# Block attention before two MLP stages: in each pair of heads the second half-tile takes the heads in the other order

## The chip, the cores and the metric

The kernel runs on one core of a Trainium2 chip. TensorE (PE) multiplies matrices, VectorE (DVE) and ScalarE (ACT) work elementwise and empty PSUM, GpSimd (POOL) does the remaining subtractions and the indirect DMAs, SyncE (SP) issues most of the DMAs. The metric is the device time of one launch in microseconds. Three runs of the kernel before took 1456.92, 1457.62 and 1458.24 us; their median is 1457.62 us.

## What is computed

Attention inside chunks of 64 positions, for 8 batches, 8 heads, 576 positions and a head size of 64; then a dense layer pair, then a layer pair of eight experts with one expert per token. Only the first part is touched:

```python
q_c, k_c, v_c = (a.reshape(B, H, nc, chunk, D) for a in (q, k, v))     # chunk = 64
scores = scale * np.matmul(q_c, k_c.transpose(0, 1, 2, 4, 3))
scores = scores - np.max(scores, axis=-1, keepdims=True)
attn = np.exp(scores)
attn = attn / (np.sum(attn, axis=-1, keepdims=True) + 1e-09)
out = np.matmul(attn, v_c)
x = out.transpose(0, 2, 1, 3).reshape(B * S, H * D)
...
h = x @ w_in;  g = s * relu(h) ** 2 + b;  y = g @ w_out
...
# expert of each token by argmax, then relu(y @ w1[e]) @ w2[e], scaled by the gate
```

## The kernel before

**Tiles and blocks.** The 4608 tokens are 36 tiles of 128 rows (two chunks of 64 each); two tiles make a block of 256 tokens, and there are 18 blocks. The 8 heads of a tile are four pairs `hp` (KC = 4). Attention of a tile has these steps: `a_transpose` (queries and keys are turned, so that the head size lies on the partitions: head 0 of a pair on partitions 0 to 63, head 1 on 64 to 127), `a_scores`, `a_soft` and `a_norm` (softmax, on DVE and ACT), `a_pt` (the probabilities are turned), `a_pv` (probabilities times values). `a_pv` leaves the result in `x0` and `x1` (a rounded high part and the rest), the moving operand of the first dense layer `l1_mm`.

**The small products.** A score or value product is 64x64x64. It occupies one quarter of the array: the row half is given by the partitions that its operands lie on, the column half by the partitions that it writes. In `a_scores` each pair makes four products, for head `r` and chunk `c`: row half `r`, column half `c`, so all four quarters come up, and the result of head `r` goes into the PSUM part `sc[r]`. In `a_pv` each pair makes four products too, for chunk `c` and head `r`: `vs` holds the values of head `r` on partition half `r`, the transposed probabilities of head `r` are on half `r` as well, and the result goes to partition half `r`. So the row half always equals the column half, and only two of the four quarters come up. All 16 results of a tile go into one PSUM tile `ps` of 128x512 f32, named `pxt`; heads 0 and 1 of one pair and chunk write the same 64 columns, on the two partition halves. Then one ACT copy (128x512) makes the high part and one DVE subtraction (128x512) the rest. Each product is an f32 matmul and stands in the trace as two matmul instructions, so that each of the two steps has 32 of them per tile.

**PSUM slots.** `pxt`, the transposed probabilities `ppt`, the small rank sums `prk` (`g_rank`), the column sums `pcs` (`c_sums`), the turned rows `pyt` and the narrow forms of the queries and keys and scores all come from one pool, `ps_1`, which has two buffers. They are given out in turn: a new tile takes the buffer of the tile given out two before it, and its first matmul waits until that one has been read.

**Order.** The program's order is written out by hand. Tiles 0 to 3 are done in a start phase in a single chain, together with the first conversions of weights (`c_split`, `c_word`, `c_high`, `c_low` on ACT and DVE, which turn double-precision weights into a high and a low part). Tiles 4 and 5 stand in a loop over `s` that still converts weights and does the dense layers of blocks 0 and 1. Then, for blocks j = 2 to 16, a loop over 16 slices `f` does the dense layers of block j (`m_l1`, `l2_lag`), the routing of block j - 1 (`gates`), the preparation of expert weights (`w_prep`, `w_high`, `w_store`) and the attention of the two tiles of block j + 1: `ATT` gives the slices. `a_pv` of the first tile stands at f = 7 ahead of `a_transpose` of the second, `a_pv` of the second at f = 13; `g_rank` of block j - 1 follows at f = 14. Block 17 and the expert stage have no attention.

Of the kernel before, what the change touches and what calls it, by code (L numbers as in the profile page):

```python
# [8 lines left out]
F32 = mybir.dt.float32  # L9
# [5 lines left out]
AF = mybir.ActivationFunctionType  # L15
ALU = mybir.AluOpType
# [14 lines left out]
def kernel(  # L31
# [16 lines left out]
    nc = tc.nc  # L48
    P = 128
# [3 lines left out]
    E, _, F2 = w1.shape  # L53
    CH = 64
    KC = DM // P
# [19 lines left out]
    def pool(name, bufs=1, side="left", st=None):  # L75
        st = st or ExitStack()
        p = st.enter_context(tc.tile_pool(name=name, bufs=bufs, side=side, reuse_waits="tile"))
        return p, st

    const, _ = pool("const", st=ctx)  # L80
# [3 lines left out]
    ps_1 = ctx.enter_context(tc.tile_pool(name="ps_1", bufs=2, space=PSUM))  # L84
# [19 lines left out]
        out=tri, in_=ones, pattern=[[1, P]], compare_op=ALU.is_gt, fill=0.0,  # L104
# [27 lines left out]
    xt_p, _ = pool("xt", 2, st=ctx)  # L132
    sm, _ = pool("sm", 2, st=ctx)
# [31 lines left out]
    def tt(out, a, b, op):  # L165
        nc.vector.tensor_tensor(out=out, in0=a, in1=b, op=op)  # L166
# [111 lines left out]
    def v_load(i, eng=None):  # L278
        if i >= NTILE:
            return  # L280
        if 0 < i < 3:
            vs = s1.tile([P, 2, KC, HD], F32, name=f"v{i}")
        else:
            vs = (s2 if i in (3, 5) else at).tile([P, 2, KC, HD], F32, tag="v", name="vs")
        for c in range(2):
            b, s = divmod(i * P + c * CH, S)
            for r in range(2):
                (eng or nc.sync).dma_start(
                    out=vs[r * CH:(r + 1) * CH, c],
                    in_=v[b, :, s:s + CH, :].rearrange("(a r) p d -> r p a d", r=2)[r],  # L290
                )
        vt[i] = vs
# [26 lines left out]
    def a_scores(i, narrow=False):  # L319
        qk = qkv[i][0]  # L320
        if narrow:
            sc = [ps_1.tile([P, KC, CH], F32, tag="p1", name="psc1") for _ in range(2)]
            parts = [(slice(r, r + 1), sc[r].unsqueeze(1)) for r in range(2)]
        else:
            ps = ps_2.tile([P, 2, 2, KC, CH], F32, tag="p2", name="psc")
            sc = [ps[:, r, 0] for r in range(2)]
            parts = [(slice(0, 2), ps[:, :, 0])]
        for hp in range(KC):
            for d in range(2):
                for r in range(2):  # L330
                    c = r ^ d
                    r0, c0 = r * CH, c * CH
                    nc.tensor.matmul(
                        sc[r][c0:c0 + CH, hp, :],
                        lhsT=qk[r0:r0 + CH, 0, hp, c0:c0 + CH],
                        rhs=qk[r0:r0 + CH, 1, hp, c0:c0 + CH],
                        start=True, stop=True,
                    )
        qkv[i][0] = parts
# [39 lines left out]
    xt = {}  # L379

    def a_pv(i):
        pt = qkv.pop(i)[1]
        vs = vt.pop(i)
        ps = ps_1.tile([P, KC, P], F32, tag="p1", name="pxt")
        for hp in range(KC):
            for c in range(2):
                for r in range(2):
                    r0, c0 = r * CH, c * CH
                    nc.tensor.matmul(
                        ps[r0:r0 + CH, hp, c0:c0 + CH],  # L390
                        lhsT=vs[r0:r0 + CH, c, hp, :],
                        rhs=pt[r0:r0 + CH, hp, c0:c0 + CH],
                        start=True, stop=True,
                    )
        j, t = divmod(i, NTB)
        if t == 0:
            xt[j] = [xt_p.tile([P, KC, TB], F32R, tag=f"x{a}", name=f"x{a}") for a in range(2)]
        hi, lo = (a[:, :, t * P:(t + 1) * P] for a in xt[j])
        nc.scalar.activation(out=hi, in_=ps, func=AF.Copy)
        tt(lo, ps, hi.bitcast(F32), ALU.subtract)  # L400


    gch = {}
# [619 lines left out]
    def att_pe(j, f, loc):  # L1023
        i = (j + 1) * NTB
        for t, (f0, f1, f2, f3, f4) in enumerate(ATT):
            narrow = i + t == 3 * NTB
            L = LOC[t]
            if f == f0 and L[0] == loc:
                a_transpose(i + t, narrow)
                a_load(i + t + 1)  # L1030
            if f == f1 and L[1] == loc:
                a_scores(i + t, narrow)
                if t:
                    drain(a_soft(i + t))
            if f == f3 and L[2] == loc:
                a_pt(i + t)
            if f == f4 and L[3] == loc:
                a_pv(i + t)
                v_load(i + t + 1)
# [57 lines left out]
    with tc.manual_schedule(engines=ENG):  # L1097
# [8 lines left out]
        c_load(0)  # L1106
        a_load(2)
        v_load(0)
        v_load(1)
        a_load(3)  # L1110
        c_load(1)
# [4 lines left out]
        nc.sync.dma_start(out=sb[:, 1:2], in_=b_in.partition_broadcast(P))  # L1116
        a_transpose(0)
        a_scores(0)
        drain(a_soft(0))
        a_transpose(1)  # L1120
        drain(a_norm(0))
        a_scores(1)
        c_split(0)
        a_pt(0)
# [3 lines left out]
        drain(a_norm(1))  # L1128
        c_high(0)
        a_pv(0)  # L1130
        c_low(0)
        v_load(2, nc.scalar)
# [3 lines left out]
        next(soft)  # L1136
        next(soft)
        a_pv(1)
        drain(soft)
        a_transpose(3)  # L1140
# [32 lines left out]
        for s in range(2, NF + LEAD + LAG):  # L1173
# [52 lines left out]
            if s == 6:  # L1226
                s1_st.close()
                wt_p, _ = pool("wt", st=ctx)
# [15 lines left out]
            if s == 17:  # L1244
                drain(c_sums(15, 16))
                su_st.close()
                y_p, _ = pool("yp", st=ctx)
                gb_p, _ = pool("gb", st=ctx)
                wgb = gb_p.tile([P, E * DM], F32, name="wgb")
                nc.sync.dma_start(  # L1250
                    out=wgb, in_=wgt.rearrange("e d -> (e d)").partition_broadcast(P)
# [4 lines left out]
        g_p, _ = pool("g", 3, st=ctx)  # L1256
# [4 lines left out]
    with tc.manual_schedule(engines=ENG):  # L1261
# [38 lines left out]
        j = NB - 1  # L1300
        xgp, _ = pool("xgp", st=ctx)
        for n in range(3):
            xg_t[n] = xgp.tile([P, ROW], F32, name=f"xg{n}")
        a1, _ = pool("a1", st=ctx)
# [3 lines left out]
        for f in range(NF):  # L1308
            if f == NF - 4:
                wi_st.close()  # L1310
                r3, _ = pool("r3", 2, st=ctx)
                r2, _ = pool("r2", st=ctx)
                uo, _ = pool("uo", st=ctx)
# [37 lines left out]
        r5, _ = pool("r5", st=ctx)  # L1351
# [8 lines left out]
        ut, _ = pool("ut", side="right", st=ctx)  # L1360
# [66 lines left out]
        hi = NU - 2  # L1427
# [49 lines left out]
```

## Time and profile before

| | us |
|---|---|
| median of three runs | 1457.62 |
| the profiled execution, its own time | 1454.87 |
| its span, first to last instruction | 1453.2 |
| PE busy, share of the span | 1408.9, 97% |
| DVE busy | 939.1, 65% |
| ACT busy | 701.0, 48% |
| mean granted clock of TensorE, share of full speed | 0.99 |

The profile is one execution on the chip. For each instruction it has the engine, the line of the kernel, the operation, the tiles and the start and end; from the semaphores it infers what ended an engine's idle time. Matmuls are pipelined, and their ends are modelled; so the cost of a row of matmuls is read from its start to the start of what follows on PE, not from its duration. PE works nearly without a gap from about 70 us on, so what shortens its work there shortens the whole, unless another engine becomes late.

### The profile page before, as it was taken

The page shows a single profiled execution, that of the slowest core. Times are in us where ns is not written, and L with a number is a line of the kernel's source. Part 1 is how long each engine was busy: PE and PEld are TensorE (multiplying, and loading weights), DVE is VectorE, ACT ScalarE, POOL GpSimd, SP SyncE. Part 2 cuts the span into 40 slices and gives each one's busy share as a digit, 9 for nine tenths or more (in the row PEclk, how much of TensorE's full clock was granted, in tenths as well). Part 3 has the DMA queues.
Part 4 walks back from the last instruction along what each step waited for, and adds up shares of the span by engine and source line. Part 5 has one row for each costly group of instructions (what it writes and reads, how often), then busy time and mean ns, then how long its engine had stood idle before and what let it go on. Part 6 is the DMA issues. An engine that isn't in the chain of part 4 may idle for free. (4 is left out here: it accounts for less than half of the span.)

```text
span 1453.2 us, 34204 instructions
## 1 busy us (share of the span) xinstructions
PE 1408.9 (97%) x13165; PEld 1184.1 (81%) x13165; DVE 939.1 (65%) x2279; ACT 701.0 (48%) x1622; POOL 448.1 (31%) x515
## 2 busy tenths in 40 slices
PE   5799999999999999999999999999999999999996
PEld 4698888888888888888888888887777777777773
DVE  5889489779778966876876786766343344344331
ACT  3786556565565555555556555543222222222221
POOL 0000232322232333233233333363543443444320
PEclk8899999999999999999999999999999999999998
DMA  7484253554545445344444534453211221535340
GB/s 174 145 200 126 100 146 115 143 151 139 144 141 149 125 120 145 112 113 126 132 124 111 152 97 118 86 176 111 74 46 52 102 100 47 181 131 196 113 149 19
DMA packets 183893, 179.00 MB, mean 123 GB/s; under 512 B 131108, under 2 KB 139556, under 8 KB 179504
## 3 DMA queue, kind: packets, MB, share of 16 engines
q1 hardware_dynamic: 171216, 157.29, 37.3%
q0 software_dynamic: 10336, 18.97, 4.2%
q8 instruction: 105, 1.72, 0.5%
q10 hardware_dynamic: 2176, 0.52, 0.2%
q14 instruction: 60, 0.49, 0.1%
HBM read 263.85 MB, written 54.14 MB: 219 GB/s over the span
## 5 line engine op out<-in xcount | busy, mean ns | idle before, releaser
L424 POOL TENSOR_TENSOR gl<-g,gh 128x256 fp32r<-128x256 f32 x256 | 222.9, 872 | 700.7 <-ACT gh L422 398.5
L409 PE MATMUL ph<-x,wi 128*128 128x256 f32 x2592 | 348.0, 285 | 5.2 <-ACT wi L232 2.7
L409 PEld LDWEIGHTS ph<-x,wi 128*128 128x128 f32 x2592 | 331.0, 191 | 20.1 <-ACT wi L232 3.4
L482 PE MATMUL py<-wo,gh 128*128 128x512 f32 x864 | 270.7, 394 | 0.0
L540 DVE CUSTOM_DVE_ANT_0 dump<-rows,wgb 128x512 bf16<-128x512 f32 x256 | 198.9, 777 | 5.0
L979 DVE CAST hh<-hr 128x512 f16<-128x512 f32 x82 | 37.4, 456 | 253.4 <-ACT hr L975 253.4
L989 PEld LDWEIGHTS <-hh 128*128 128x128 f16 x984 | 94.6, 98 | 106.7
L419 ACT ACTIVATE g<-ph 128x256 f32<-128x256 f32 x256 | 97.2, 380 | 165.1 <-PE ph L409 156.9
L975 ACT ACTIVATE hr<-pu,scu 128x128 f32<-128x128 f32 x328 | 93.5, 367 | 169.9 <-PE pu L967 87.2
L482 PE MATMUL py<-wo,gl 128*128 128x512 f32 x432 | 170.5, 395 | 0.0
L482 PEld LDWEIGHTS py<-wo,gh 128*128 128x128 f32 x864 | 148.1, 188 | 20.9
L967 PEld LDWEIGHTS <-wa 128*128 128x128 f16 x2208 | 127.0, 98 | 5.5 <-issue 0.3
L967 PE MATMUL pu<-xhl,wa 128*128 128x128 f16 x2208 | 130.6, 219 | 0.0
L718 DVE SCALAR_TENSOR_TENSOR hl<-raw,wup,hl 128x512 f16<-128x512 f32 x128 | 106.7, 873 | 30.8 <-ACT hl L711 30.8
L989 PE MATMUL po<-wa,hh 128*128 128x512 f16 x552 | 122.9, 379 | 0.0
L409 PE MATMUL ph<-x,wj 128*128 128x256 f32 x864 | 116.0, 284 | 1.8 <-DVE wj L166 1.8
L711 ACT ACTIVATE hl<-raw,wup 128x512 f16<-128x512 f32 x128 | 85.1, 711 | 62.3 <-DVE wup L163 40.4
L409 PEld LDWEIGHTS ph<-x,wj 128*128 128x128 f32 x864 | 108.1, 189 | 6.3 <-DVE wj L166 2.0
L996 POOL DMA_INDIRECT out_dram<-o,uid x41 | 42.1, 1028 | 225.0 <-ACT o L995 211.6
L420 ACT ACTIVATE g<-g 128x256 f32<-128x256 f32 x256 | 107.0, 418 | 8.1
L422 ACT ACTIVATE gh<-g 128x256 fp32r<-128x256 f32 x256 | 107.0, 418 | 8.1
L995 ACT ACTIVATE o<-po,scu 128x512 f32<-128x512 f32 x41 | 28.2, 687 | 164.4 <-PE po L989 164.4
(210 smaller groups left out, 2031.3 us busy)
## 6 DMA issues: line engine op xcount, KB each, us to landing
wa<-wd SPq DMA_DIRECT2D x64, 1024.0 KB
wb<-wd SPq DMA_DIRECT2D x60, 1024.0 KB
raw<-in_moe_w_dram SPq DMA_DIRECT2D x64, 512.0 KB
wd<-hl SPq DMA_DIRECT2D x128, 256.0 KB
wb<-wd SPq DMA_DIRECT2D x20, 1030.5 KB
wa<-wd SPq DMA_DIRECT2D x20, 1030.5 KB
ys<-rows SPq DMA_DIRECT2D x18, 513.0 KB
vs<-in_v_dram SPq DMA_DIRECT2D x132, 64.0 KB
```

The source lines that it names most:

```text
L409: nc.tensor.matmul(ps, lhsT=wi_f(a, f)[:, kc], rhs=xt[j][b][:, kc, :], start=(n == 0), stop=(n == 3 * KC - 1),)
L419: nc.scalar.activation(out=g, in_=ps, func=AF.Relu)
L420: nc.scalar.activation(out=g, in_=g, func=AF.Square)
L422: nc.scalar.activation(out=hi, in_=g, func=AF.Copy)
L424: nc.gpsimd.tensor_tensor(out=lo, in0=g, in1=hi.bitcast(F32), op=ALU.subtract)
L482: nc.tensor.matmul(yps[j][t], lhsT=g[a][:, t * P:(t + 1) * P], rhs=wo_f(b, f), start=(f == 0 and n == 0), stop=(f == NF - 1 and n == 2),)
L540: nc.vector.tensor_tensor_reduce(out=dump, in0=ysb[j][:, t, :DM], in1=wgb[:, e * DM:(e + 1) * DM], scale=1.0, scalar=0.0, op0=ALU.mult, op ...
L711: nc.scalar.activation(out=hl[:, 0], in_=raw[:, a], func=AF.Copy, scale=sc)
L718: nc.vector.scalar_tensor_tensor(out=hl[:, 1], in0=raw[:, a], scalar=sc, in1=hl[:, 0], op0=ALU.mult, op1=ALU.subtract)
L967: nc.tensor.matmul(ps[:, f, :], lhsT=w[:, kc, a, f * P:(f + 1) * P], rhs=hl[:, b, kc, :], start=(n == 0), stop=(n == 3 * KC - 1),)
L975: nc.scalar.activation(out=r[:, f, :], in_=ps[:, f, :], func=AF.Relu, scale=scu[:, c:c + 1])
L989: nc.tensor.matmul(ps, lhsT=hh[:, a, c, :], rhs=w[:, c % 4, b, :], start=(n == 0), stop=(n == 3 * NC2 - 1),)
```

## The change

The values of the chunk c = 1 are loaded with the two heads of a pair exchanged: head `r` lies on partition half `r ^ c`. To match, the scores go into the part `sc[d]`, with d = r ^ c, in place of `sc[r]`; so in chunk 1 the two heads of a pair change places in the softmax tile, and after the transposition head `r` of chunk `c` lies on half `r ^ c`. In `a_pv` the operands are taken from half `k0` = (r ^ c) * 64, and the result still goes to half `r`. The products of chunk 0 lie in the quarters in which row half and column half are the same, those of chunk 1 in the two others. The results of the two chunks go into two PSUM tiles of 128x256, both of the pool `ps_1`, and each has its own ACT copy and its own DVE subtraction. Nothing is computed in addition.

```diff
@@ v_load
             for r in range(2):
                 (eng or nc.sync).dma_start(
-                    out=vs[r * CH:(r + 1) * CH, c],
+                    out=vs[(r ^ c) * CH:(r ^ c) * CH + CH, c],
                     in_=v[b, :, s:s + CH, :].rearrange("(a r) p d -> r p a d", r=2)[r],
                 )
@@ a_scores
                     c = r ^ d
                     r0, c0 = r * CH, c * CH
                     nc.tensor.matmul(
-                        sc[r][c0:c0 + CH, hp, :],
+                        sc[d][c0:c0 + CH, hp, :],
                         lhsT=qk[r0:r0 + CH, 0, hp, c0:c0 + CH],
                         rhs=qk[r0:r0 + CH, 1, hp, c0:c0 + CH],
@@ a_pv
-        ps = ps_1.tile([P, KC, P], F32, tag="p1", name="pxt")
+        ps = [ps_1.tile([P, KC, CH], F32, tag="p1", name="pxt") for _ in range(2)]
         for hp in range(KC):
             for c in range(2):
                 for r in range(2):
-                    r0, c0 = r * CH, c * CH
+                    r0, c0, k0 = r * CH, c * CH, (r ^ c) * CH
                     nc.tensor.matmul(
-                        ps[r0:r0 + CH, hp, c0:c0 + CH],
-                        lhsT=vs[r0:r0 + CH, c, hp, :],
-                        rhs=pt[r0:r0 + CH, hp, c0:c0 + CH],
+                        ps[c][r0:r0 + CH, hp, :],
+                        lhsT=vs[k0:k0 + CH, c, hp, :],
+                        rhs=pt[k0:k0 + CH, hp, c0:c0 + CH],
                         start=True, stop=True,
                     )
@@
-        hi, lo = (a[:, :, t * P:(t + 1) * P] for a in xt[j])
-        nc.scalar.activation(out=hi, in_=ps, func=AF.Copy)
-        tt(lo, ps, hi.bitcast(F32), ALU.subtract)
+        for c in range(2):
+            c0 = t * P + c * CH
+            hi, lo = (a[:, :, c0:c0 + CH] for a in xt[j])
+            nc.scalar.activation(out=hi, in_=ps[c], func=AF.Copy)
+            tt(lo, ps[c], hi.bitcast(F32), ALU.subtract)
```

No instruction passes another, but since `a_pv` now takes two slots of `ps_1`, some matmuls wait for other readers than before. Two places show it; the words in square brackets are the engines and DMA queues whose semaphores an instruction waits for. The first is PE at the value product of tile 5, in the loop over `s`, before and after:

```order
L243 MATMUL pcs_1707<-wt0_879,one_157 128x512 [waits Activation_49]
L243 MATMUL pcs_1707<-wt1_880,one_157 128x512
L389 MATMUL pxt_1721<-pt_1672,vs_1101 64x64 [waits DVE_49]
L389 MATMUL pxt_1721<-pt_1672,vs_1101 64x64
L389 MATMUL pxt_1721<-pt_1672,vs_1101 64x64 [waits DMAHW1_49]
L389 MATMUL pxt_1721<-pt_1672,vs_1101 64x64 [waits DMAHW2_49]
L389 MATMUL pxt_1721<-pt_1672,vs_1101 64x64 x12
```

```order
L243 MATMUL pcs_1722<-wt0_891,one_157 128x512 [waits Activation_49]
L243 MATMUL pcs_1722<-wt1_892,one_157 128x512
L391 MATMUL pxt_1736<-pt_1687,vs_1113 64x64 [waits DVE_49]
L391 MATMUL pxt_1736<-pt_1687,vs_1113 64x64
L391 MATMUL pxt_1737<-pt_1687,vs_1113 64x64 [waits DMAHW1_49,DVE_49]
L391 MATMUL pxt_1737<-pt_1687,vs_1113 64x64 [waits DMAHW2_49]
L391 MATMUL pxt_1736<-pt_1687,vs_1113 64x64 x2
L391 MATMUL pxt_1737<-pt_1687,vs_1113 64x64 x2
```

The second of the two tiles, `pxt_1737`, takes the buffer that `pcs` has just filled, and its first matmul waits for DVE, which reads `pcs`. The second place is PE at `g_rank` of block 1, at f = 14 of j = 2, after the value product of tile 7:

```order
L631 LDWEIGHTS ones_85
L631 MATMUL prk_2486<-run_1960,ones_85 128x8 [waits PE_49]
L632 LDWEIGHTS tri_87
L632 MATMUL prk_2486<-oh_2392,tri_87 128x8 [waits DVE_49]
L631 LDWEIGHTS ones_85
L631 MATMUL prk_2486<-run_2394,ones_85 128x8 [waits DVE_49]
```

```order
L635 LDWEIGHTS ones_85
L635 MATMUL prk_2510<-run_1978,ones_85 128x8 [waits DVE_49]
L636 LDWEIGHTS tri_87
L636 MATMUL prk_2510<-oh_2413,tri_87 128x8
L635 LDWEIGHTS ones_85
L635 MATMUL prk_2510<-run_2415,ones_85 128x8
```

Before, `prk` took the buffer of `ppt`; now it takes that of the first `pxt` tile, so its first matmul waits for DVE to have subtracted from it. The same stands in every block from j = 2 to 16.

## Rows read from the trace of the kernel before

**Rows 1.** The page, part 1: busy time of each engine over the span.
```profile
PE 1408.9 (97%) x13165; PEld 1184.1 (81%) x13165; DVE 939.1 (65%) x2279; ACT 701.0 (48%) x1622; POOL 448.1 (31%) x515
```
**Rows 2.** Busy time by stretches of the span; the first line names the columns.
```profile
core 0: us, PE busy (x) PEld busy (x) DVE busy (x) ACT busy (x) POOL busy (x), PEclk, DMA share, GB/s
...
20.00:30.00 10.00, 3.52 (x40) 3.41 (x41) 1.58 (x4) 2.10 (x4) 0.00 (x0) 0.51 0.72 232
...
50.00:60.00 10.00, 7.82 (x47) 6.45 (x46) 8.75 (x16) 9.90 (x20) 0.00 (x0) 0.95 0.53 167
...
200.00:400.00 200.00, 199.16 (x1696) 176.71 (x1695) 164.48 (x417) 118.09 (x264) 60.37 (x69) 1.00 0.52 143
...
930.00:1453.20 523.20, 507.38 (x5458) 384.06 (x5456) 219.41 (x522) 149.45 (x435) 208.84 (x235) 0.99 0.33 106
```
**Rows 3.** Timeline, PE, 249 to 267 us: start, duration, line, tiles, count [idle].
```profile
249.98 1.15 PE L389 MATMUL pxt<-pt,vs 64*64 64x64 f32 x32
251.06 1.69 PE L409 MATMUL ph<-x,wj 128*128 128x256 f32 x12
...
265.53 0.69 PE L333 MATMUL psc<-qk 64*64 64x64 f32 x32 [0.46 <-DVE qk L316]
266.16 0.73 PE L482 MATMUL py<-wt,gh 128*128 128x512 f32 x2
```
**Rows 4.** Matmuls started by 250.08 us (L389) and 265.56 us (L333): count, durations, starts.
```profile
L389 PE MATMUL pxt<-pt,vs x2: 267/267/267, 250.0 to 250.0; 64*64 64x64 f32 x2
...
L333 PE MATMUL psc<-qk x4: 267/267/267, 265.5 to 265.6; 64*64 64x64 f32 x4
```
**Rows 5.** Groups by line and shape: count, busy us, mean ns of one, idle before.
```profile
L419 ACT ACTIVATE g<-ph 128x256 f32<-128x256 f32 x256 | 97.2, 380 | 165.1 <-PE ph L409 156.9 <-POOL gl L424 5.9 <-PE prk L634 0.2
...
L166 DVE TENSOR_TENSOR x<-pxt,x 128x512 fp32r<-128x512 f32 x36 | 24.7, 687 | 36.7 <-ACT x L399 36.6
...
L399 ACT ACTIVATE x<-pxt 128x512 fp32r<-128x512 f32 x36 | 21.2, 589 | 17.2 <-PE pxt L389 17.2
...
L166 DVE TENSOR_TENSOR pr<-psc,mx 128x256 f32<-128x256 f32 x6 | 2.2, 412 | 0.0
```
**Rows 6.** Timeline, 251 to 256 us: DVE's subtraction, and PE's next use of the pool.
```profile
251.81 0.69 DVE L166 TENSOR_TENSOR x<-pxt,x 128x512 fp32r<-128x512 f32 x1
...
255.35 0.18 PE L631 MATMUL prk<-run,ones 128*128 128x8 bf16 x1
```
**Rows 7.** Timeline, DVE and PE at the value product of tile 5.
```profile
151.80 0.69 DVE L166 TENSOR_TENSOR cb<-pcs,cb 128x512 f32<-128x512 f32 x1 [2.27 <-PE pcs L243]
...
151.69 1.15 PE L389 MATMUL pxt<-pt,vs 64*64 64x64 f32 x32
152.77 0.73 PE L482 MATMUL py<-wt,gh 128*128 128x512 f32 x2
```
**Rows 8.** Timeline, DVE and PE, tiles 6 and 7 in block j = 2.
```profile
180.37 0.69 DVE L316 COPY qk<-pqk 128x512 f32<-128x512 f32 x1 [0.31 <-ACT qk L312]
...
203.64 0.69 DVE L166 TENSOR_TENSOR x<-pxt,x 128x512 fp32r<-128x512 f32 x1
...
203.20 0.18 PE L631 MATMUL prk<-run,ones 128*128 128x8 bf16 x1
...
203.63 0.71 PE L482 MATMUL py<-wt,gh 128*128 128x512 f32 x2
```
**Rows 9.** Timeline, PE and ACT in the start phase.
```profile
7.34 1.14 PE L333 MATMUL psc<-qk 64*64 64x64 f32 x32 [0.88 <-DVE qk L316]
...
25.83 0.60 ACT L376 ACTIVATE pt<-ppt 128x512 f32<-128x512 f32 x1 [7.74 <-DMA v<-in_v_dram]
26.48 1.97 PE L389 MATMUL pxt<-pt,v 64*64 64x64 f32 x32 [7.78 <-ACT pt L376]
...
40.22 1.09 PE L372 MATMUL ppt<-ident,pr 128*128 128x128 f32 x4 [3.27 <-DVE pr L166]
...
46.31 0.50 PE L409 MATMUL ph<-x,wi 128*128 128x256 f32 x2 [1.22 <-ACT wi L232]
```

## The prediction

> **What bounds the kernel now.** I read the busy times first, then the stretches, then the timeline around the changed steps, then the start phase. PE is busy for 97% of the span [rows 1]. By stretches it is busy for 199.16 of the 200 us from 200 to 400 us, at full granted clock, while DVE has 164 us of work there and ACT 118 us [rows 2]. All but the first six tiles have their attention in this regime, up to 926 us. So a microsecond taken from PE there is a microsecond of the whole, as long as DVE and ACT are still in time where PE waits for them. The expert stage after 930 us is PE's too [rows 2] and is not touched: it only starts earlier. The first 70 us are different. PE is idle for much of them, its clock falls to a mean of 0.51 in one stretch, and from 50 to 60 us ACT is the full engine [rows 2].
>
> **The value product itself.** In the steady part a value product takes from 249.98 to 251.06 us on PE, 1.08 us. A score product, with the same count and shape of matmuls, takes from 265.53 to 266.16 us, 0.63 us [rows 3]. The difference shows at the front of each: within the first 0.1 us two value matmuls have started, but four score matmuls [rows 4]. 32 matmuls two at a time are 16 groups, four at a time 8 groups, so the 0.45 us of difference are 8 groups of 0.056 us each. The scores use four quarters of the array and the values two; after the change the values use four as well, in the order of the scores (two on the diagonal, then two off it). I therefore give the value product the 0.63 us of the scores: **0.45 us less per tile**.
>
> Does the new placing of results stand against that? Now the two diagonal products of a pair write the same columns of one PSUM tile, on the two partition halves, and the two others do so in a second tile; that holds for the scores as well, which before kept each row half to its own part. The nearest row is the old value product: its heads 0 and 1 write the same columns of `pxt` on the two halves, and both start within the first 0.1 us [rows 4], with the next pair right behind, as 1.08 us for 16 groups say. So two row halves do write into one place at the same time. No row shows this with four in flight. Taken as it stands, the price is 0; at the other end it is 0.45 us per tile for the scores, and no gain for the values (the first rival).
>
> [...]
>
> **Emptying PSUM.** One ACT copy of 128x512 (589 ns) becomes two of 128x256, near 380 ns by the nearest row from PSUM; one DVE subtraction (687 ns) becomes two of about 412 ns [rows 5]. That is 0.17 us more on ACT and 0.14 us more on DVE per tile, 6 and 5 us over 36 tiles. In the steady part both hide behind PE: DVE has 35 us to spare in 200 [rows 2]. And the result is not later: DVE begins after the first, short copy, and the last half is ready after 0.38 + 0.41 + 0.41 = 1.20 us in place of 0.59 + 0.69 = 1.28 us. The loads of the values are the same four DMAs with other target partitions, at no cost.
>
> **The slots.** A value product now takes both buffers of the pool. In blocks 3 to 16 the next use after the second tile's product is the rank sum, and it now waits for DVE's first subtraction. That subtraction starts at 251.81 us, and even the whole of it ends at 252.50 us; the rank sum comes at 255.35 us [rows 6]. The 2.85 us of cover shrink by the 0.45 us saved at most, so the cost is nothing. The scores of the next tile already wait 0.46 us for DVE in one such block [rows 3]; the chain that delays them starts behind the value product and moves with it, so I leave that wait as it is. So **28 tiles (8 to 35) give 28 x 0.45 = 12.6 us**.
>
> Three places are worse. *Tile 5*: its second PSUM tile takes the buffer of the column sums. DVE reads these from 151.80 to 152.49 us, and the value product starts at 151.69 us [rows 7]. The third product must wait until about 152.54 us, 0.85 us after the first; nearly the whole product still follows it, so PE goes on after about 0.85 + 0.63 = 1.48 us where it took 1.08 us: **0.4 us lost** instead of 0.45 us gained. *Tiles 6 and 7*: from 180.37 us to past 204 us DVE works almost without a break, and PE's next needs come out of that row of work. It starts at a copy that waited 0.31 us for ACT [rows 8]; an earlier value product of tile 6 can bring it forward by at most these 0.31 us, less 0.14 us of longer subtraction ahead of it; I take 0.2 us. At its end DVE subtracts tile 7 at 203.64 us, then 203.44 us, and the first half is done at 203.85 us. The rank sum, which began at 203.20 us and let PE go on at 203.63 us [rows 8], now starts at 203.9 us and lets PE go on at 203.98 us. Both tiles together: **0.35 us lost** rather than 0.9 us gained. *Tile 4* has no such neighbour: 0.45 us gained.
>
> **The start phase.** Tile 0: nothing, because ACT is held until 25.83 us by the loads of values [rows 9]. Tile 1 runs while the granted clock is near its lower level (0.51 from 20 to 30 us [rows 2]): 1.97 us, against 1.14 us for scores run that slowly [rows 9], so 0.83 us less, and ACT's next work hangs on it; 0.7 us after ACT's longer copies. Tile 2: the probabilities of tile 3 wait 3.27 us for DVE [rows 9], whose chain begins at this value product: 0.5 us. Tile 3: PE waits for converted weights after it [rows 9], so nothing is gained; there ACT is full [rows 2], and the longer copies cost 0.2 us. Sum 1.0 us gained. As idle PE also moves the granted clock here, I bound it by 0.5 us lost and 2.5 us gained.
>
> **The sum.** 12.6 + 0.45 - 0.4 - 0.35 + 1.0 = 13.3 us. The profiled execution took 1454.87 us, of which 1453.2 us are span, and would take 1441.6 us. It lies 2.75 us below the median of the runs; from the median the forecast is 1457.6 - 13.3 = **1444.3 us**.
>
> **The rivals.**
>
> *Slower, through PSUM.* With four quarters in flight, two row halves that write one tile get in each other's way. Then the scores fall from 0.63 to 1.08 us, and the values stay at 1.08 us: 36 x 0.45 = 16 us more, about 1474 us. It decides as soon as the pair on the diagonal and the pair off it cannot be written together; if it only halves the overlap of both, gain and loss cancel near 1457 us. For it: the scores before kept each row half to its own part, and no row has four in flight in the new way. Against it: the pairs of the old value product. Chance 0.07.
>
> *No four in flight.* The third matmul of each value product carries a new wait, and the loads of the values are waited for one by one; if that keeps the pairs apart, the value product stays at 1.08 us. Then only the losses of tiles 5 to 7 and the start phase remain: 1457 to 1459 us. Against it: the waits are for things long done in the steady part, and the old product had the waits for the loads too. Chance 0.05.
>
> *The slots cost more.* DVE's subtraction comes late not in one block only but in many, because DVE is filled with routing ahead of it. Each block in which the rank sum then waits as in block 2 loses what its second tile gains and 0.35 us more, 0.8 us; seven of the 14 blocks would cost 5.6 us, hence 1450 us, all of them 1455 us. Against it: the 2.85 us of cover [rows 6]. Chance 0.08.
>
> **How the numbers follow.** The forecast keeps 0.80. Its own bounds: at the low end all 36 tiles give 0.45 us and the start phase 1.0 us besides, 17.2 us, 1440.4 us; at the high end a start phase 1.5 us worse than taken and a tenth of the steady gain lost to handing over between products, 10.5 us, 1447 us. The range reaches 1 us below, for a run with a higher clock in the start phase, and up to 1450.5 us to take in the nearer half of the third rival: 1439.5 to 1450.5 us. About 0.2% (2.9 us) is what a measurement of this kernel can tell from no change. Faster by more than that: 0.80 + 0.07 of the third rival = 0.87. Within it: 0.05 + 0.01 = 0.06. Slower: 0.07.
>
> **What would show it.** In the profile of the changed kernel, the steady value product should take 0.63 us to the next start, with four matmuls started in the first 0.1 us, and the scores should still take 0.63 us. The copies should be near 0.38 us and the subtractions near 0.41 us. PE should wait about 0.8 us inside the value product of tile 5, and for DVE ahead of the rank sum of block 1 only. The forecast is wrong if the scores get longer, if the rank sums wait in later blocks, or if the first 70 us change by more than 2.5 us.

## The result and the profile after

The changed kernel takes **1443.11 us** (median of four runs, 1441.65 to 1445.47) against 1457.27 us for the kernel before in the same comparison: ratio 0.9904, 95% interval 0.9890 to 0.9917. The forecast was 1444.3 us. The profiled execution took 1441.65 us, 13.2 us less than the one of before.

The timeline of PE around the value product of tile 9 and the score product of tile 10, as in [rows 3] (start, duration, line, tiles, count):

```profile
247.57 0.69 PE L391 MATMUL pxt<-pt,vs 64*64 64x64 f32 x32
248.20 0.97 PE L413 MATMUL ph<-x,wj 128*128 128x256 f32 x6
...
262.23 0.69 PE L335 MATMUL psc<-qk 64*64 64x64 f32 x32
262.86 0.50 PE L486 MATMUL py<-wt,gh 128*128 128x512 f32 x1
```

The value product now takes 0.63 us from its start to the next matmul, where it took 1.08 us; the score product still takes 0.63 us. The matmuls of the same value product that have started within the first 40 ns, as in [rows 4]:

```profile
L391 PE MATMUL pxt<-pt,vs x4: 267/267/267, 247.6 to 247.6; 64*64 64x64 f32 x4
```

Four, where there were two. The groups of the page and by shape that empty PSUM, as in [rows 1, 5]:

```profile
PE 1391.7 (97%) x13165; PEld 1166.9 (81%) x13165; DVE 942.6 (65%) x2315; ACT 703.2 (49%) x1658; POOL 448.4 (31%) x515
```

```profile
L166 DVE TENSOR_TENSOR x<-pxt,x 128x256 fp32r<-128x256 f32 x72 | 27.0, 416 | 19.4 <-ACT x L403 19.4
...
L403 ACT ACTIVATE x<-pxt 128x256 fp32r<-128x256 f32 x72 | 23.2, 373 | 9.9 <-PE pxt L391 9.9
```

The halves take 416 and 373 ns; DVE and ACT have 3.5 and 2.2 us more work in all. And the waits of PE (waiting tile and line, who is waited for, us in total, times, longest):

```profile
PE psc L335 <- DVE qk L316: 1.8, 2, 1.0
...
PE ppt L374 <- DVE x L166: 1.7, 1, 1.7
PE prk L635 <- DVE x L166: 1.2, 1, 1.2
...
PE px L952 <- DMA xg<-ys,uid: 0.9, 1, 0.9
PE psc L335 <- ACT qk L314: 0.8, 1, 0.8
PE pxt L391 <- DVE cb L166: 0.5, 1, 0.5
PE pqk L307 <- DVE rows L495: 0.5, 1, 0.5
```

Five of these are new: `ppt`, `prk` and `pxt` wait for a slot of the pool, each once; `pqk` waits once for DVE's `rows`; and a score product of the start phase waits once for ACT's `qk`.

How far the second profile is ahead of the first, by the starts of value products:

| place | before, us | after, us | ahead by | gained since the row above |
|---|---|---|---|---|
| tile 4 starts | 137.88 | 135.31 | 2.57 | 2.57 (start phase) |
| tile 5 starts | 151.69 | 148.66 | 3.03 | 0.46 (tile 4) |
| tile 6 starts | 177.53 | 174.82 | 2.71 | -0.32 (tile 5) |
| tile 8 starts | 229.73 | 227.78 | 1.95 | -0.76 (tiles 6 and 7) |
| what follows tile 35 starts | 926.50 | 912.01 | 14.49 | 12.54 (tiles 8 to 35) |
| end of the span | 1453.2 | 1439.9 | 13.3 | -1.2 (expert stage) |

### The profile page after: what moved, and what is told of

Same layout as the page of the kernel before. It is cut to its first block, busy times and chain, and to the rows that moved or that the text cites. A ratio compares the mean times of both kernels' runs of the same rounds, so it can differ in the third digit from the quotient of the medians.

```text
span 1439.9 us, 34299 instructions
## 1 busy us (share of the span) xinstructions
PE 1391.7 (97%) x13165; PEld 1166.9 (81%) x13165; DVE 942.6 (65%) x2315; ACT 703.2 (49%) x1658; POOL 448.4 (31%) x515
## 5 line engine op out<-in xcount | busy, mean ns | idle before, releaser
L722 DVE SCALAR_TENSOR_TENSOR hl<-raw,wup,hl 128x512 f16<-128x512 f32 x128 | 111.1, 908 | 30.3 <-ACT hl L715 30.3
```

The costliest lines, as they stand in the source:

```text
L722: nc.vector.scalar_tensor_tensor(out=hl[:, 1], in0=raw[:, a], scalar=sc, in1=hl[:, 0], op0=ALU.mult, op1=ALU.subtract)
```

## Experiments

**The theory**: the matmuls of one quarter start one after the other, 58 ns apart (the distance of neighbouring starts of one quarter within the value product of tile 9, before and after, at a granted clock of 1.00; only the second comes 0.11 us behind the first), and the gain is that four quarters work at once where two did. The trace gives a product the size 64*64 and no place in the array; a quarter here is the pair of operand half and result half. The score products of the kernel before come in four such pairs, and their matmuls start four at a time, within 0.03 us of one another. **Rivals**: the gain comes from emptying PSUM in two halves; or from where operands and results lie; or the start phase makes much of it by chance.

**One part alone: two PSUM tiles, no exchange of heads** (on the kernel before).

```diff
-        ps = ps_1.tile([P, KC, P], F32, tag="p1", name="pxt")
+        ps = [ps_1.tile([P, KC, CH], F32, tag="p1", name="pxt") for _ in range(2)]
...
-                        ps[r0:r0 + CH, hp, c0:c0 + CH],
+                        ps[c][r0:r0 + CH, hp, :],
...
+        for c in range(2):
...
+            nc.scalar.activation(out=hi, in_=ps[c], func=AF.Copy)
+            tt(lo, ps[c], hi.bitcast(F32), ALU.subtract)
```

> One part alone: two PSUM tiles per value product, with their own copies and subtractions, but the heads stay where they were before, so that only two quarters of the array come up. Theory of the quarters: the value product stays at 1.08 us to the next start in the steady part, two matmuls started in the first 0.1 us; the slots cost what they cost in the changed kernel or a little more (a wait inside the value product of tile 5, one ahead of the rank sum of block 1, together about 1.3 us); time 1457 to 1460 us, ratio 1.000 to 1.002 to the kernel before. Rival (the gain comes from emptying PSUM in two shorter halves): the time falls as in the changed kernel, to about 1443 us, ratio 0.990.

Measured: 1456.32 us against 1455.57 us, ratio 1.0005 (0.9995 to 1.0014). The timeline of PE at the value product of tile 9, and the matmuls started within its first 60 ns:

```profile
252.34 1.15 PE L389 MATMUL pxt<-pt,vs 64*64 64x64 f32 x32
253.42 0.39 PE L411 MATMUL ph<-x,wj 128*128 128x256 f32 x1
```

```profile
L389 PE MATMUL pxt<-pt,vs x2: 267/267/267, 252.3 to 252.3; 64*64 64x64 f32 x2
```

1.08 us and two at a time. Two tiles and shorter copies alone give nothing that these runs can tell; the ratio lies where it was expected, and the time 0.7 us under the expected range (in this comparison the kernel before takes less, too). The extra waits for slots (0.5 us at `pxt`, 0.7 us at `prk` in this profile) are no larger than the interval of the runs. No run has the other part alone, heads exchanged and one PSUM tile; so whether four quarters would work at once into one tile, and the split is needed, stays open.

**The same products in another order** (on the changed kernel): first all of chunk 0, whose quarters are the two on the diagonal, then all of chunk 1.

```diff
-        for hp in range(KC):
-            for c in range(2):
+        for c in range(2):
+            for hp in range(KC):
                 for r in range(2):
```

> The changed kernel with one loop exchanged: in the value product all products of chunk 0 (both on the diagonal) stand ahead of all of chunk 1 (both off it). The same instructions, operands and results, but neighbours share two quarters. Theory of the quarters: 16 groups of two again, the value product takes about 1.08 us, and the steady gain of 0.45 us a tile is lost: 1455 to 1459 us, ratio 0.998 to 1.001. Rival (what counts is where operands and results lie, not which products are neighbours): 0.63 us, about 1443 us, ratio 0.990.

Measured: 1448.66 us, ratio 0.9952 (0.9935 to 0.9969): half of the gain is lost, not all of it. The value product of tile 9 on PE, and the matmuls of it that had started 0.29 us (first line), 0.305 us (second line) and 0.515 us (third line) after its beginning:

```profile
248.26 0.98 PE L391 MATMUL pxt<-pt,vs 64*64 64x64 f32 x32
249.17 0.38 PE L413 MATMUL ph<-x,wj 128*128 128x256 f32 x1
```

```profile
L391 PE MATMUL pxt<-pt,vs x10: 218/218/267, 248.3 to 248.5; 64*64 64x64 f32 x10
...
L391 PE MATMUL pxt<-pt,vs x12: 218/218/267, 248.3 to 248.6; 64*64 64x64 f32 x12
...
L391 PE MATMUL pxt<-pt,vs x22: 218/218/267, 248.3 to 248.7; 64*64 64x64 f32 x22
```

0.91 us, between 0.63 and 1.08 us. Ten have started by 0.29 us, as many as five pairs, and within 15 ns more two others start. The trace has one name for both PSUM tiles, so that these two are of chunk 1 is read from the distance: in one quarter starts lie 58 ns apart. Up to the 22nd both chunks run side by side; the last ten come in pairs again. Each quarter has eight matmuls, so chunk 0 still had six to go when chunk 1 began. The order is what counts, and not the placing alone, since operands and results lie as in the changed kernel; but matmuls of chunk 1 started while six of chunk 0, three in each quarter, had not.

**The same exchange in the scores** (on the changed kernel): all products on the diagonal first.

```diff
-        for hp in range(KC):
-            for d in range(2):
+        for d in range(2):
+            for hp in range(KC):
                 for r in range(2):
```

> The changed kernel with the same exchange in the score product: first all products on the diagonal, then all off it. Theory of the quarters: the score product goes from 0.63 to about 1.08 us in every tile and the value product stays at 0.63 us; 36 x 0.45 = 16 us more than the changed kernel, 1457 to 1461 us. Rival (the pitch of the score product is set by the issue of matmuls or by waiting for its operands): it stays at 0.63 us, about 1443 us.

Measured: 1448.01 us, ratio 0.9948 (0.9932 to 0.9964). The timeline of PE at the score product of tile 10:

```profile
262.09 0.97 PE L333 MATMUL psc<-qk 64*64 64x64 f32 x32 [0.19 <-DVE qk L316]
263.00 0.50 PE L484 MATMUL py<-wt,gh 128*128 128x512 f32 x1
```

0.91 us as well, so the size was missed in the same way and the direction held: what the values gained, the scores lose in part as soon as their neighbours share quarters. The value product stays at 0.63 us in this profile.

**Sorted by quarter** (on the changed kernel), to see how many matmuls of a busy quarter have not started when the next quarter begins:

```diff
-        for hp in range(KC):
-            for c in range(2):
-                for r in range(2):
+        for c in range(2):
+            for r in range(2):
+                for hp in range(KC):
```

> The changed kernel with the products of the value step sorted by quarter: all four of one quarter, then all four of the next. Same instructions and results. From the exchange of loops, where products of a free quarter started while six matmuls of the busy ones were still waiting, I expect a quarter to start when six or fewer are pending ahead of it: 18 groups in place of 8, about 1.2 us for the value product, some 20 us more in all (1460 to 1465 us). Without any overtaking it would be 32 groups, 1.9 us or more, and some 45 us more. Rival (only the placing counts): 0.63 us.

Measured: 1535.1 us, one run, against 1517.14 us for the kernel before on the same chip, hence 30 us more than the changed kernel there (1505.36 us, below). The value product of tile 9 on PE, and the matmuls started 0.283 and 0.288 us after its beginning:

```profile
251.79 1.54 PE L391 MATMUL pxt<-pt,vs 64*64 64x64 f32 x32
253.25 0.38 PE L413 MATMUL ph<-x,wj 128*128 128x256 f32 x1
```

```profile
L391 PE MATMUL pxt<-pt,vs x5: 218/218/267, 251.8 to 252.1; 64*64 64x64 f32 x5
...
L391 PE MATMUL pxt<-pt,vs x6: 218/218/267, 251.8 to 252.1; 64*64 64x64 f32 x6
```

1.46 us, where 1.2 us was expected. Here five have started by 0.283 us and the sixth by 0.288 us; less than 58 ns behind the fifth, it is read as the first of the second quarter, and it starts when the first quarter has three to go, not six. One count fits both orders: three matmuls of each busy quarter had not started when the next quarter began. An estimate from it: if the 32 matmuls in four blocks overlap by three at each of three borders, they make 32 - 9 = 23 groups of 58 ns, 15 more than the 8 of the changed kernel; 15 x 0.058 = 0.87 us, and 0.63 + 0.87 = 1.50 us, near the 1.46 us. By the same count the exchange of loops has 16 - 3 = 13 groups, 5 more than 8, and 0.63 + 5 x 0.058 = 0.92 us, where 0.91 us was measured. The count was made after both runs, to fit them; no run made for it tests it, and what sets it is not shown.

**The changed kernel again, and the kernel before again.** These and the next two runs look at the start phase. The chip on which the kernel before takes 1517 us spends some 60 us more in the expert stage (591 us behind tile 35 in the changed kernel's profile there, 528 us in its first profile), 40 us of it as waits of PE for issue in each profile taken there, so times there are compared with one another alone.

> The kernel before once more, for a second profile of its start phase. If the 2.5 us by which the changed kernel's start phase is shorter belong to the change, the score product of tile 4 starts again near 110.7 us (within 0.5 us) and the granted clock of the first 60 us looks the same; if they are in part the clock's, that start differs by 1 us or more between the two profiles of one kernel.

> The changed kernel once more, beside the next three on one chip, for a second profile and more runs. The steady part should be the same to 0.1 us per block; the score product of tile 4, which started at 108.27 us, may move by about 1 us, as it did between two profiles of the kernel before (110.73 and 109.68 us). Time 1442 to 1445 us.

Measured: the changed kernel 1505.36 us against 1517.14 us, ratio 0.9913 (0.9884 to 0.9943). The score product of tile 4, once per profile, in this order: before, before again, after, after again:

```profile
110.73 0.46 PE L333 MATMUL psc<-qk 64*64 64x64 f32 x16
```

```profile
109.68 0.52 PE L333 MATMUL psc<-qk 64*64 64x64 f32 x20
```

```profile
108.27 0.69 PE L335 MATMUL psc<-qk 64*64 64x64 f32 x32
```

```profile
109.47 0.64 PE L335 MATMUL psc<-qk 64*64 64x64 f32 x28
```

(The counts are those of the part of the product that the asked stretch holds.) Each kernel's start phase moves by more than 1 us from one profile to the next.

**The change from tile 4 on only** (on the changed kernel).

```diff
-                    out=vs[(r ^ c) * CH:(r ^ c) * CH + CH, c],
+                    out=vs[(r ^ (c if i > 3 else 0)) * CH:(r ^ (c if i > 3 else 0)) * CH + CH, c],
...
-                        sc[d][c0:c0 + CH, hp, :],
+                        sc[d if i > 3 else r][c0:c0 + CH, hp, :],
...
+        new = i > 3
...
-                    r0, c0, k0 = r * CH, c * CH, (r ^ c) * CH
+                    r0, c0, k0 = r * CH, c * CH, (r ^ (c if new else 0)) * CH
...
```

> The change from tile 4 on; tiles 0 to 3 as they were before (old placing, one PSUM tile, one copy). If the gain of the start phase belongs to the change, the score product of tile 4 starts near 110.2 us, between the two profiles of the kernel before, and the time is 1.5 to 2.5 us above the changed kernel's; if it was the clock's in the one profile, the start lies anywhere from 108 to 110.7 us and the runs are within 0.5 us of the changed kernel's. The steady part gains 0.45 us a tile either way.

Measured: 1505.06 us, ratio 0.9917 (0.9893 to 0.9941): no difference from the changed kernel that these runs can tell, though with intervals of 0.24% to each side they could not tell the 1.5 to 2.5 us of the one case from the 0.5 us of the other. Its score product of tile 4, in the timeline of PE:

```profile
109.26 0.45 PE L335 MATMUL psc<-qk 64*64 64x64 f32 x15
```

So of the 2.57 us that the first pair of profiles shows for the start phase, most is not shown to be the change's. With the old start phase that start was at 110.73, 109.68, 109.26 and (two tiles only) 110.30 us, with the new placing and order at 108.27, 109.47 and, in the next run, 108.89 us. The means, 110.0 and 108.9 us, are 1.1 us apart, no more than the spread within either, and both chips are mixed in them. The other orders spread wider: 107.16 us with the chunks one after the other, whose value products are slower than the changed kernel's, 107.47 us with the scores exchanged, 110.40 us sorted by quarter.

One part of the start phase is steady, the value product of tile 1 ([rows 9] has it before). The timeline of PE, first in the changed kernel, then in this one:

```profile
26.47 1.23 PE L391 MATMUL pxt<-pt,v 64*64 64x64 f32 x32 [7.40 <-ACT pt L378]
27.64 1.11 PE L307 MATMUL pqk<-ident,q 128*128 128x128 f32 x4
```

```profile
25.29 1.97 PE L396 MATMUL pxt<-pt,v 64*64 64x64 f32 x32 [6.64 <-ACT pt L378]
27.19 1.12 PE L307 MATMUL pqk<-ident,q 128*128 128x128 f32 x4
```

From its start to the next matmul it takes 1.90 us in all four profiles in which tile 1 has the old quarters (the kernel before twice, two tiles only, and this one) and 1.16 us in all four with the new placing and order of the values. These 0.74 us are the change's; how much of them reaches tile 4 is not shown.

**The rank sum of block 1 one slice later** (on the changed kernel), so that DVE is ahead of it.

```diff
-                if f == RANK:
+                if f == (15 if j == 2 else RANK):
                     g_rank(j - 1)
...
-        if f == DEST:
+        if f == (15 if j == 1 else DEST):
             r.append(g_dest(j))
```

> The changed kernel with the rank sum of block 1 (and what DVE makes of it) one slice later, behind the next 2.8 us of matmuls, so that DVE has subtracted from the PSUM tile before PE comes to it. If the 1.2 us wait ahead of that rank sum is a net loss, it is gone (below 0.1 us) and everything behind it starts 1.0 to 1.2 us earlier relative to the value product of tile 7 (29.6 to 29.8 us from there to the rank-sum-free value product of tile 8's block, 32.58 us to tile 8's own before); the runs can hardly tell 0.08%. Rival: the wait moves to the next thing that DVE owes PE, and nothing is gained.

Measured: 1503.26 us, ratio 0.9902 (0.9878 to 0.9925). The timeline of PE at the rank sum, first in the changed kernel's second profile, then in this kernel:

```profile
202.26 0.17 PE L635 MATMUL prk<-run,ones 128*128 128x8 bf16 x1 [1.15 <-DVE x L166]
```

```profile
202.99 0.18 PE L635 MATMUL prk<-run,ones 128*128 128x8 bf16 x1
```

The wait is gone, and none has taken its place: from the value product of tile 7 to that of tile 8 it is 31.19 us (195.25 to 226.44 us), against 32.51 us (195.99 to 228.50 us). That is 1.3 us less than in the changed kernel, a little more than expected, and the lead is still 1.3 us behind tile 35. The runs, with intervals of 0.2 to 0.3% to each side, do not tell the two apart.

## Why the prediction was right, point by point

**The value product.** Forecast 0.45 us less per tile, measured 0.45 us (1.08 to 0.63 us). The reason given was the number of quarters in flight, and the runs bear it out from both sides: the split alone leaves two at a time and gains nothing, and bad neighbours take a part of the gain away while all placing stays. That two row halves write the same columns of one tile, on different partition halves, costs nothing with four in flight either: the score product stays at 0.63 us with its parts exchanged. So the first rival is out. That two row halves write the same partitions of one PSUM part was not tried.

**28 tiles, 12.6 us.** Measured 12.54 us in the first pair of profiles, but that close a hit is luck. The products alone give 28 x 0.454 = 12.7 us. From block 7 to block 16 a block gains only 0.80 or 0.85 us, not the 0.91 us of its two products. A part of the difference lies between value product and rank sum, which are 0.05 us further apart in each block (4.34 us from the one's end to the other's start, before 4.29 us), where I had put nothing. That the rank sum now waits for another reader does not explain it: with two tiles alone it waits for the same reader, and the distance is 4.29 us; the cause stays open. In the first pair most of this is made up by waits of two score products for DVE, 0.7 us in all ([rows 3] has one), which are gone in the profile after. But such waits come and go from one profile of a kernel to the next: the second of the kernel before has none here, the second of the changed kernel one of 0.5 us. In the second profile of the kernel before the stretch from tile 8 to what follows tile 35 takes 696.06 us, not 696.76 us; with the value product and the scores of the changed kernel it takes 684.23 to 684.64 us in four profiles. The gain is therefore 11.4 to 12.5 us.

**Emptying PSUM.** One half takes 416 and 373 ns (412 and 380 ns forecast), but the two halves overlap in the trace: the busy time of these subtractions rose from 24.7 to 27.0 us, that of the copies from 21.2 to 23.2 us, 0.06 us per tile on either engine where 0.14 and 0.17 us were forecast. In the steady part both hide behind PE: from 200 to 400 us of the profile after PE is busy for 198.65 us, DVE for 166.55 us and ACT for 119.81 us. The loads of the values, forecast at no cost, took SP a median of 608 ns an issue before and after.

**The slots.** *Tile 5*: forecast that the third product waits until 0.85 us after the first and that the whole takes 1.48 us; the timelines of PE and DVE:

```profile
148.66 0.33 PE L391 MATMUL pxt<-pt,vs 64*64 64x64 f32 x4
149.52 0.68 PE L391 MATMUL pxt<-pt,vs 64*64 64x64 f32 x28 [0.52 <-DVE cb L166]
150.13 0.50 PE L486 MATMUL py<-wt,gh 128*128 128x512 f32 x1
```

```profile
148.77 0.69 DVE L166 TENSOR_TENSOR cb<-pcs,cb 128x512 f32<-128x512 f32 x1 [2.27 <-PE pcs L243]
```

0.86 us and 1.47 us. *Tile 7*: the rank sum waited 1.16 us for the subtraction that DVE began at 201.01 us, and PE went on 6.38 us after the value product's start, 0.58 us later than before; the forecast amounts to 6.35 us (203.98 us less a start 0.2 us ahead of the old 197.83 us), so this place is right. It is the only rank sum that waits for the subtraction (1.2 us, once, in the list of waits above), so the rival of slots that cost more in many blocks is out. *Tile 6* is where the step failed: I had 0.2 us gained through DVE's row of work. The timelines of PE and DVE show another wait:

```profile
174.82 0.69 PE L391 MATMUL pxt<-pt,vs 64*64 64x64 f32 x32
176.02 0.44 PE L307 MATMUL pqk<-ident,qs 128*128 128x128 f32 x2 [0.50 <-DVE rows L495]
```

```profile
174.55 1.41 DVE L495 SCALAR_TENSOR_TENSOR rows<-py,sb,cb 128x512 f32<-128x512 f32 x2 [2.74 <-DMA ys<-rows]
```

The turned queries take the PSUM tile of block 1's results, which DVE can empty only when the DMA of the rows of block 0 has landed. So the product of tile 6 gained nothing, and 0.12 us were lost. From tile 6 to tile 8 the table has 0.76 us lost, where 0.35 us was forecast. In the second profile of the changed kernel the product of tile 6 took 0.75 us in place of 1.19 us.

**The start phase.** Forecast 1.0 us, with bounds of -0.5 and 2.5 us; 2.57 us in the first pair of profiles, just outside, 1.1 us by the means above. The order of size fits; that it is the change's is shown for the 0.74 us at tile 1 alone, where 0.83 us was forecast. The bounds were set for a granted clock that moves with PE's idle time. In the first pair of profiles it falls within the longest gap of PE (18.70 to 26.48 us before, 19.07 to 26.47 us after) and comes back behind it: 0.57 and 0.74 from 20 to 22 us, 0.50 in both from 22 to 30 us, 1.00 in both from 32 to 34 us. That the one causes the other is not shown.

**The end.** 1.2 us of the lead were lost after 926 us, which the sum did not have. Between the two profiles of the kernel before the same stage differs by 1.1 us (the second is 1.7 us ahead at tile 35 and 0.6 us at the end), so this is no effect of the change that can be told.

**The sum.** 13.3 us forecast; 13.3 us between the spans and 14.2 us between the medians. The errors (1.6 us more in the start phase, 0.4 us less at tiles 6 and 7, 1.2 us less at the end) cancel, so that agreement to 0.1 us is luck; what stands on firm ground is the 0.45 us per value product and, of it, 11.4 to 12.5 us in 28 tiles.

## What to carry to other kernels

When two steps have the same matmuls and one takes 1.08 us where the other takes 0.63 us, look at how many start at once at the front of each: here products of one quarter started 58 ns apart and four of four quarters within 0.03 us, so operands and results were laid out so that four neighbours in the program lie in four quarters (with the results in two PSUM tiles; one tile was not tried). A step that takes two slots of a ring of two makes the next user wait for its readers; name that reader for each place, because where DVE is behind it can cost more than the step gained: at tile 7 the rank sum waited 1.16 us, where the value product had gained 0.45 us, and in one profile a slice of distance took that wait away and 1.3 us with it. When a start phase with a moving clock lies ahead (here 0.50 to 1.00 in stretches of 2 us), compare several profiles before a microsecond there is put down to a change.

## What was not expected of the hardware

PE did not hold back the matmuls of free quarters until the busy ones were done. The kernel before shows it by name in its start phase. In the program all of the value product of tile 0 stands ahead of the score product of tile 2; on PE two matmuls of the second start 0.05 us before the last two of the first:

```profile
17.11 0.27 PE L333 MATMUL psc<-qk 64*64 64x64 f32 x2
17.16 0.22 PE L389 MATMUL pxt<-pt,vs 64*64 64x64 f32 x2
17.22 0.63 PE L333 MATMUL psc<-qk 64*64 64x64 f32 x30
```

In the experiments, with two quarters busy, matmuls of the other two started while six earlier ones had not; with one busy, while three had not. By the estimate above that is why the exchange of two loops cost 0.28 us a tile (0.91 against 0.63 us) and not 0.45 us, and why sorting by quarter cost 0.83 us (1.46 against 0.63 us) and not much more.
